# Part of the attention sum moved from VectorE to accumulating DMAs in a planned one-core kernel

## The chip, the cores and the metric

The kernel runs on one core of a Trainium2 chip. The core has a matrix engine (TensorE, PE in the profile, with its weight loads as PEld), a vector engine (VectorE, DVE), an engine for element functions and copies (ScalarE, ACT), a general one (GpSimd, POOL) and one that only issues transfers (SyncE, SP). Sixteen DMA engines move data. DMAs can be issued from SP, ACT and POOL; each of these takes its instructions in order. A DMA with `accum_op=ALU.add` adds what it reads to what lies at its destination; in this kernel all of those are issued from POOL.

The metric is device time in microseconds (us), as the median of several runs. Before the change it is 262.89 (three runs, 261.79 to 262.96).

## The reference

A block of a transformer with its two halves side by side. `x` is 2048 positions of 640 values, in bfloat16.

```python
xn = layernorm(x)                            # over the 640 values
q, k, v = split(xn @ wqkv)                   # 32 heads of 20
# attention: each position sees 8 positions: itself and 2, 4, ... 14 before it
logits[s, w] = sum_d q[s, d] * k[s - 2 * w, d] * 20 ** -0.5     # -1e9 where s - 2 * w < 0
o[s, :] = sum_w softmax(logits)[s, w] * v[s - 2 * w, :]
out = x + o @ wo + ((xn @ w_gate) * (xn @ w_up)) @ w_down       # 1536 inner values
```

## The kernel before

**Tiles and chunks.** The 2048 positions are 16 tiles of 128, and 4 chunks of 4 tiles (512 positions). Per chunk the kernel does, in this order on TensorE: the q and k projections (`qk`, L419), the v projection (`vproj`, L452), the gate and up products (`glu`, L677: 12 blocks f, each with 5 matmuls for gate and 5 for up), and the down projection (`down`, L728) with the output projection of the attention added into the same bank (L731). Chunks overlap: q, k and v of chunk c+2 are made after `down` of chunk c, so the attention of a chunk has most of a stage's time on the other engines.

**Attention of a chunk c.** VectorE multiplies q with shifted k (`products`, L520): 8 products, two into each of four buffers `pw`. Each product still has 5 blocks of 128 lanes to be summed per head. `fold` (L496) sums blocks on VectorE, in steps: a first one from 5 blocks to 3 (128x2048), a second to 2 and a third to 1 (128x1024 each); `LEVELS[c]` says how many steps. What is left is summed by TensorE in `logits` (L537), with a constant matrix `Ek`: 4 matmuls per block that is left. There are two groups of logits in a chunk, g = 0 and 1, each over two of the `pw` buffers. ScalarE copies the result out of PSUM (L552), and a transposing DMA, issued from SP, turns it into `LT` with positions on the partitions. Then VectorE takes the maximum (L578 to L582), ScalarE the exponential (L587), VectorE normalises (L595 to L600), twice per chunk, for two tiles each.

**The weighted sum over the 8 offsets.** For each tile, `av(t)` loads 8 shifted copies of v into a buffer `v8` (128 x 8 x 640, from the DRAM tensor `vD`, issued from SP, 1280 KB). VectorE weights them (L635, 128x5120), adds copies 4 to 7 to 0 to 3 (`tree`, L644, 128x2560), and then 2 to 2 and 1 to 1 (`tree2`, L648, L650). The result is transposed by a DMA from SP to `oT`, which `down` needs. `pw` and `v8` share five buffers named `pv`.

**Around it.** `vproj` evicts v from PSUM on ScalarE (L458) into one of three buffers `v_t`, and POOL stores it to `vD` (L473). The layer norm has its statistics on VectorE (L251 to L259), the power and, from tile 8 on, a shift `ns` on POOL (L265, L312) and the application on VectorE or, from tile 8 on, on ScalarE (L315). VectorE makes `hT` = gate x up (L693), 12 per chunk; TensorE starts `down` of a chunk's first tile when 10 of them are there, and needs the last two some 4 us later. For tiles 0 to 13 `out` is first seeded with x, chunk by chunk (`seed`, L709, DRAM to DRAM, from POOL), and `y` is then added to it by an accumulating DMA (L772, from POOL; the buffers `y` are two). Tiles 14 and 15 take x into SBUF (`load_xr`, L703) and are added on VectorE.

**What sets the order.** The code first collects steps, each with an engine, a cost, an occupation of the engine, what it depends on and what it must come after; `Plan.order` (L48) then places them in a list, engine by engine, always the step that is ready, with the earliest due time first. A step marked `urgent` (the logits) goes before all others that are ready, and `margin` lets what follows on another engine count as ready only so much later. The order that results is what the engines get; on the chip each engine takes its instructions in that order and waits where an input is not there yet. PE's matmuls other than the logits form one chain (`pe_main`).

Of the kernel before, what the change touches and what calls it, by code (L numbers as in the profile page):

```python
# [31 lines left out]
class Plan:  # L32
# [8 lines left out]
    def add(self, eng, cost, fn, deps=(), occ=None, after=(), kb=0):  # L41
        s = Step(eng, cost, fn, deps, occ, after)
        s.kb = kb
        s.idx = len(self.steps)
        self.steps.append(s)
        return s
# [51 lines left out]
def kernel(  # L98
# [381 lines left out]
    FO = {}  # L480
    PW, LL, LE, SS, DD, AA, O16, OE, V8, DT = {}, {}, {}, {}, {}, {}, {}, {}, {}, {}

    LEVELS = (1, 2, 3, 3)
    FOLDER = ('DVE', 'DVE', 'DVE', 'DVE')
    LEFT = (tuple(range(KT)), (0, 1, KT - 1), (0, KT - 1), (0,))
    HALVES = ((0, 2, 2, 4), (0, 1, 1, 2), (0, 1, KT - 1, KT))
# [19 lines left out]
    def products(c, hf):  # L506
        for j in range(4):
            i = 4 * hf + j
            u = i // 2

            def mul(u=u, j=j):
                if j % 2 == 0:
                    new(("pw", c, u), [P, 4, KT, HS], BF, "pv", 5)
                o = T["pw", c, u][:, 2 * (j % 2) : 2 * (j % 2) + 2, :, :]
                lo = hf * HS
                qh = T["q", c][:, :, lo : lo + HS]
                kh = T["k", c][:, :, lo + DIL * j : lo + DIL * j + HS]
                qh = bass.AP(tensor=qh.tensor, offset=qh.offset, ap=[list(qh.ap[0]), [0, 2], *[list(x) for x in qh.ap[1:]]])
                kh = bass.AP(tensor=kh.tensor, offset=kh.offset, ap=[list(kh.ap[0]), [4 * DIL, 2], *[list(x) for x in kh.ap[1:]]])
                nc.vector.tensor_tensor(o, qh, kh, ALU.mult)  # L520

            m = 8 * c + i
            w = [LL.get(2 * c - 1), O16.get(4 * c - 4), O16.get(4 * c - 3), O16.get(4 * c - 2)][u]
            PW[m] = add("DVE", 1.48, mul, [*Q[c], *Kk[c], w], occ=1.395, after=[PW.get(m - 1) if i else V8.get(4 * c - 1)])
            if j % 2:
                FO[4 * c + u] = fold(c, u)
        LASTPW[c] = PW[m]

    def logits(c, g):
        n = 2 * c + g  # L530

        def lg():
            l = new(("lps", c, g), [P, 512], F32, "pl", 2, psum)
            left = LEFT[LEVELS[c]]
            for i in left:
                for j in range(4):
                    nc.tensor.matmul(l[H * j : H * (j + 1), :], lhsT=Ek[:], rhs=T["pw", c, 2 * g + j // 2][:, 2 * (j % 2) : 2 * (j % 2) + 2, i, :],  # L537
                                     start=(i == left[0]), stop=(i == left[-1]), tile_position=(0, H * j),
                                     skip_group_check=True)

        took = 0.022 + 0.2195 * len(LEFT[LEVELS[c]])
        LL[n] = add("PE", took + 0.13, lg, [FO[2 * n], FO[2 * n + 1], LL.get(n - 1), LE.get(n - 2), CE], occ=took)
        LL[n].urgent = True
        LL[n].margin = 0.9

        def ev():
            L = new(("L", c, g), [P, 2, 2, P], BF, "L", 2)
            ps = T["lps", c, g]
            if n == 0:
                head = ps[:].rearrange("p (o s) -> p o s", o=2)[:, :, 0:HALO]  # L550
                nc.vector.tensor_tensor(head, head, negm[:], ALU.add)
            nc.scalar.copy(L[:].rearrange("p t o s -> p o t s"), ps[:].rearrange("p (o t s) -> p o t s", o=2, t=2))  # L552

        LE[n] = add("ACT", 0.585, ev, [LL[n], SS.get(n - 2), CM], occ=0.5)

        def tr():
            lt = new(("LT", n), [P, 2, W, H], BF, "LT", 2)
            out = lt[:].rearrange("p t (o w) h -> p (t o) (w h)", o=2)
            nc.sync.dma_start_transpose(out=out, in_=T["L", c, g][:].rearrange("p t o s -> p (t o s)"))

        early = [SPLAST[0]] if c == 0 else []
        SS[n] = SPLAST[0] = add("SP", 3.5, tr, [LE[n], DD.get(n - 2)], occ=1.25, after=early, kb=160)
# [62 lines left out]
    def load_out():  # L625
        WL["o"] = SPLAST[0] = add("SP", 8, wo_load, after=[SPLAST[0]], occ=2.7, kb=1100)

    def av(t):
        n, u = divmod(t, 2)
        if t > 2:  # L630
            load_v8(t)

        def mul():
            v = T["v8", t]
            nc.vector.tensor_tensor(  # L635
                v[:].rearrange("p w (j h) -> p w j h", j=Dh, h=H),
                v[:].rearrange("p w (j h) -> p w j h", j=Dh, h=H),
                T["a", n][:, u, :, None, :].to_broadcast([P, W, Dh, H]),
                ALU.mult,
            )  # L640

        def tree():
            v = T["v8", t]
            nc.vector.tensor_tensor(v[:, 0:4, :], v[:, 0:4, :], v[:, 4:8, :], ALU.add)  # L644

        def tree2():
            v = T["v8", t]
            nc.vector.tensor_tensor(v[:, 0:2, :], v[:, 0:2, :], v[:, 2:4, :], ALU.add)  # L648
            o = new(("o", t), [P, D], BF, "o", 2)
            nc.vector.tensor_tensor(o[:], v[:, 0, :], v[:, 1, :], ALU.add)  # L650

        a = add("DVE", 2.82, mul, [AA[n], V8[t]], occ=2.735)
        b = add("DVE", 1.485, tree, [a], occ=1.4)

        def tr():
            o = new(("oT", t), [P, KT, P], BF, "oT", 4)
            nc.sync.dma_start_transpose(out=o[:], in_=T["o", t][:])

        O16[t] = add("DVE", 1.35, tree2, [b, OE.get(t - 2)], occ=1.26)
        OE[t] = add("SP", 2.8, tr, [O16[t], DT.get(t - 4)], occ=1.3, kb=200, after=[V8[2]])  # L660
        if t == 0:
            SPLAST[0] = OE[0]
            load_out()
# [32 lines left out]

    XR, OB, CP = {}, {}, {}
    DIRECT = NT - 2

    def load_xr(t):  # L700
        def fn():
            x = new(("xr", t), [P, D], BF, "x", 5)
            nc.gpsimd.dma_start(out=x[:], in_=x_flat[t * P : (t + 1) * P, :])  # L703
        XR[t] = add("POOL", 2.6, fn, [VS[6]], occ=0.5, after=[HT[t // CH, 3 + t % CH]])

    def seed(c):
        def fn():
            rows = slice(c * CS, min((c + 1) * CS, DIRECT * P))
            nc.gpsimd.dma_start(out=out_flat[rows, :], in_=x_flat[rows, :])  # L709
        CP[c] = add("POOL", 6.0, fn, [VS[6]], occ=0.6, after=[HT[c, 3]])  # L710

    def down(t):
        c, q = divmod(t, CH)
        if t >= DIRECT:
            load_xr(t)
        if q == 0:
            seed(c)
        evs = []
        last = t == NT - 1
        at = [0, 512, D] if last else [0, NS, D]  # L720
# [107 lines left out]
    def between(c, work):  # L828
        for q in range(CH):
            work(q)  # L830
            if c < NCH:
                ln(c * CH + q)
                transposes(c * CH + q)
# [18 lines left out]
    for c in range(NCH):  # L852
        attention(c)
        glu(c)
        between(c + 2, lambda q: down(c * CH + q))
        if c + 2 < NCH:
            halo(c + 2)
            qk(c + 2, 0, CS)
            for q in range(CH):
                vproj((c + 2) * CH + q)  # L860
# [33 lines left out]
```

## Time and profile before

One execution was profiled. Its time was 263.27 us, of which the span from the first to the last instruction is 261.6; the granted TensorE clock was 1.000 throughout.

| what | value |
|---|---|
| median of the runs | 262.89 us |
| profiled execution, and its span | 263.27 us, 261.6 us |
| DVE: product L520 (32 times) | 1485 ns each |
| DVE: weighting L635 (16) | 2820 ns |
| DVE: first sum over offsets L644 (16) | 1486 ns |
| DVE: later sums L648, L650 (16 each) | 822, 492 ns |
| DVE: fold of 128x2048 and of 128x1024 (16, 20) | 1218, 683 ns |
| POOL: store of y, issue, and to landing (14) | 879 ns, 3.6 to 7.3 us |
| SP: load of v8, to landing (16) | 10.1 us, median |
| POOL: seed of `out`, to landing (4) | 5.1 to 12.5 us |
| DMA queues' share of the 16 engines, SP and POOL | 50.6%, 16.5% |

How to read it: the page gives each engine's busy time, then the chain of work that ended last, then groups of instructions by line. A duration on VectorE includes some 0.08 us in which the next instruction, if it does not need the result, has already begun. A bracket such as [0.77 <-ACT v_t L458] is idle time of the engine before that instruction, with what ended it. A busy TensorE has matmuls that overlap, so the distance from one start to the next is used for sums: 0.216 us for 512 columns, 0.136 for 320.

### The profile page before, as it was taken

Reading aid. Unit: us, or ns where it says so; the run is one execution under the profiler, and the core shown is the slowest. Engines: PE = TensorE matmul, PEld = TensorE weight load, DVE = VectorE, ACT = ScalarE, POOL = GpSimd, SP = SyncE. Lnnn points to the kernel's source line nnn. Section 1 sums busy time; section 2 is a strip of 40 time slices with the busy share of each in tenths; the row PEclk is TensorE's granted clock in tenths of the full one; section 3 lists DMA queues with packets and bytes.
Section 4 is the critical chain, followed back from the end, with each engine's and each line's share of the span. In section 5 each row is a group of like instructions: output and inputs, shape, how many; then the busy total and the mean of one; then the engine's idle time right before and its main releaser. Section 6 shows DMA issues by size and latency. Waiting matters only on the chain.

```text
span 261.6 us, 3920 instructions
## 1 busy us (share of the span) xinstructions
PE 252.9 (97%) x1451; PEld 141.3 (54%) x1470; DVE 229.9 (88%) x336; ACT 121.7 (47%) x233; POOL 44.8 (17%) x82
## 2 busy tenths in 40 slices
PE   6999999999999999899999999999999999999795
PEld 2655555444677546344477745544457744445563
DVE  5883998999999999799999987999999953999971
ACT  2657566856221468675521167275532144752100
POOL 4541004200042116700011110210001230000110
DMA  7998994999998505997149536971154369940361
GB/s 210 343 200 262 397 325 121 393 351 255 227 179 208 93 20 160 379 257 81 28 84 224 97 45 212 379 259 25 25 143 110 29 93 221 363 141 3 44 82 50
DMA packets 51507, 46.54 MB, mean 178 GB/s; under 512 B 24626, under 2 KB 49472, under 8 KB 51424
## 3 DMA queue, kind: packets, MB, share of 16 engines
q1 hardware_dynamic: 46704, 37.10, 50.6%
q0 software_dynamic: 3184, 8.05, 16.5%
q10 hardware_dynamic: 1600, 1.15, 1.4%
q8 instruction: 11, 0.18, 0.3%
q14 instruction: 8, 0.07, 0.1%
HBM read 35.39 MB, written 7.55 MB: 164 GB/s over the span
## 4 chain that ended last, share of the span: by engine, by line
PE 57%; DVE 30%; DMA 9%; issue 2%; ACT 1%; POOL 0%; SPq 0%; ACTq 0%
PE ps L677 18%; PE ps L728 14%; PE ps L419 12%; DVE pv L635 7%; PE ps L731 6%; PE ps L452 5%; DVE pv L520 4%; DMA LT<-L 4%; DVE pv L644 3%; DMA vD<-v_t 3%; DVE pv L496 3%; DVE hT L693 3%; DVE pv L648 2%; DMA x<-in_A_x_dram 2%; DVE st L251 2%
## 5 line engine op out<-in xcount | busy, mean ns | idle before, releaser
L677 PE MATMUL ps<-xnT,wg 128*128 128x512 bf16 x230 | 59.1, 379 | 1.3 <-ACT v_t L458 0.8
L677 PE MATMUL ps<-xnT,wu 128*128 128x512 bf16 x238 | 59.5, 379 | 0.1
L728 PE MATMUL ps<-wd,hT 128*128 128x320 bf16 (+2 forms) x383 | 57.7, 299 | 1.7 <-DVE hT L693 1.6
L520 DVE TENSOR_TENSOR pv<-q,k 128x2560 bf16<-128x2560 bf16 x32 | 45.7, 1485 | 4.4 <-ACT k L426 4.4
L728 PEld LDWEIGHTS <-hT 128*128 128x128 bf16 x384 | 37.1, 98 | 18.1 <-DVE hT L693 2.5
L635 DVE TENSOR_TENSOR pv<-pv,a 128x5120 bf16<-128x5120 bf16 x16 | 45.1, 2820 | 0.1
L677 PEld LDWEIGHTS <-wg 128*128 128x128 bf16 x240 | 23.2, 98 | 29.1 <-issue 1.9
L677 PEld LDWEIGHTS <-wu 128*128 128x128 bf16 x240 | 23.5, 98 | 28.3
L743 ACT COPY y<-ps 128x320 f32<-128x320 f32 x28 | 11.5, 427 | 54.6 <-PE ps L731 32.2
L682 ACT CAST us<-ps 128x512 bf16<-128x512 f32 x48 | 28.3, 590 | 17.1 <-PE ps L677 17.0
L682 ACT CAST gs<-ps 128x512 bf16<-128x512 f32 x48 | 28.3, 591 | 16.8 <-PE ps L677 16.7
L772 POOL DMA_DIRECT2D out_dram<-y x14 | 12.3, 879 | 120.0 <-ACT y L743 119.6
L496 DVE TENSOR_TENSOR pv<-pv 128x1024 bf16<-128x1024 bf16 (+1 forms) x36 | 30.9, 921 | 0.0
L731 PE MATMUL ps<-wo,oT 128*128 128x320 bf16 (+2 forms) x160 | 27.0, 299 | 0.0
L644 DVE TENSOR_TENSOR pv<-pv 128x2560 bf16<-128x2560 bf16 x16 | 23.8, 1486 | 0.1
L452 PE MATMUL ps<-wv,xnT 128*128 128x320 bf16 x160 | 23.2, 299 | 0.4 <-ACT xnT L365 0.4
L693 DVE TENSOR_TENSOR hT<-gs,us 128x512 bf16<-128x512 bf16 x48 | 19.3, 419 | 4.1 <-ACT us L682 4.1
L419 PE MATMUL ps<-xnT,wk 128*128 128x512 bf16 x98 | 22.6, 380 | 0.1
L419 PE MATMUL ps<-xnT,wq 128*128 128x512 bf16 x96 | 22.2, 379 | 0.2
L452 PEld LDWEIGHTS <-xnT 128*128 128x128 bf16 x160 | 15.3, 98 | 7.3 <-ACT xnT L365 0.5
L731 PEld LDWEIGHTS <-oT 128*128 128x128 bf16 x160 | 15.5, 98 | 6.2
L419 PEld LDWEIGHTS <-wk 128*128 128x128 bf16 x100 | 11.5, 118 | 10.3 <-issue 1.1
(59 smaller groups left out, 194.8 us busy)
## 6 DMA issues: line engine op xcount, KB each, us to landing
pv<-vD SPq DMA_DIRECT2D x16, 1280.0 KB, 10.1
vD<-v_t POOLq DMA_DIRECT2D x16, 160.0 KB, 5.2
out_dram<-y POOLq DMA_DIRECT2D x14, 160.0 KB, 3.9
wg<-in_B_w_gate_dram SPq DMA_DIRECT2D x1, 1920.0 KB, 8.0
wu<-in_B_w_up_dram SPq DMA_DIRECT2D x1, 1920.0 KB, 12.3
wd<-in_B_w_down_dram SPq DMA_DIRECT2D x1, 1920.0 KB, 12.3
out_dram<-in_A_x_dram POOLq DMA_DIRECT2D x3, 640.0 KB, 6.7
x<-in_A_x_dram SPq DMA_DIRECT2D x11, 160.0 KB, 4.8
```

The costliest lines, as they stand in the source:

```text
L419: nc.tensor.matmul(T[key][:, 0:n], lhsT=(wk if r else wq)[:, i, :].rearrange("p (c b) -> p c b", b=KT)[:, :, j], rhs=T["xnT", c][:, i, lo ...
L452: nc.tensor.matmul(T["psv", t, n][:, 0:NS], lhsT=T["xnT", c][:, i, q * P : (q + 1) * P], rhs=wv[:, i, n * NS : (n + 1) * NS], start=(i == ...
L496: nc.vector.tensor_tensor(w[:, :, lo:hi, :], w[:, :, lo:hi, :], w[:, :, a:b, :], ALU.add)
L520: nc.vector.tensor_tensor(o, qh, kh, ALU.mult)
L635: nc.vector.tensor_tensor(v[:].rearrange("p w (j h) -> p w j h", j=Dh, h=H), v[:].rearrange("p w (j h) -> p w j h", j=Dh, h=H), T["a", n][ ...
L644: nc.vector.tensor_tensor(v[:, 0:4, :], v[:, 0:4, :], v[:, 4:8, :], ALU.add)
L677: nc.tensor.matmul(ps[:], lhsT=(wu if r else wg)[:, i, f * P : (f + 1) * P], rhs=T["xnT", c][:, i, :], start=(i == 0), stop=(i == KT - 1))
L682: nc.scalar.copy(s[:], T[key][:])
L693: nc.vector.tensor_tensor(h[:], T["gs", c, f][:], T["us", c, f][:], ALU.mult)
L728: nc.tensor.matmul(ps, lhsT=T["hT", c, f][:, q * P : (q + 1) * P], rhs=wd[:, f, sl], start=(f == 0), stop=(f == FT - 1 and not wo_part))
L731: nc.tensor.matmul(ps, lhsT=T["oT", t][:, g, :], rhs=wo[:, g, sl], start=False, stop=(g == KT - 1 and f1 == FT))
L772: nc.gpsimd.dma_start(out=out_flat[t * P : (t + 1) * P, :], in_=T["y", t][:], accum_op=ALU.add)
```

## The change

Five edits:

1. The first sum over the offsets (`tree`) of tiles 4 to 14 is no longer made by VectorE but by two accumulating DMAs from POOL, each adding 128 x 2 x 640 values inside the buffer `v8`. Tiles 0 to 3 and 15 stay as they are.
2. The products of chunk 1 are folded to one block, as those of chunks 2 and 3 are (`LEVELS`).
3. In chunks 1 to 3 the first group of logits also waits for the folds of the second, so the two follow each other on TensorE; the planner's costs and margins for them change. In every chunk the fifth product comes after the folds of the second buffer.
4. Seeds of chunks 1 to 3 are issued a stage earlier: a one-element copy on POOL (`gate`) waits for the ninth `hT` of the chunk before.
5. The loads of x for tiles 14 and 15 come after the last seed.

```diff
-    LEVELS = (1, 2, 3, 3)
+    LEVELS = (1, 3, 3, 3)
...
-            PW[m] = add("DVE", 1.48, mul, [*Q[c], *Kk[c], w], occ=1.395, after=[PW.get(m - 1) if i else V8.get(4 * c - 1)])
+            PW[m] = add("DVE", 1.48, mul, [*Q[c], *Kk[c], w], occ=1.395, after=[(FO[4 * c + 1] if i == 4 else PW.get(m - 1)) if i else V8.get(4 * c - 1)])
...
+    PAIRED = (1, 2, 3)
...
-        took = 0.022 + 0.2195 * len(LEFT[LEVELS[c]])
-        LL[n] = add("PE", took + 0.13, lg, [FO[2 * n], FO[2 * n + 1], LL.get(n - 1), LE.get(n - 2), CE], occ=took)
+        alone = not (g and c in PAIRED)
+        took = 0.022 + 0.2195 * len(LEFT[LEVELS[c]]) + (0.19 if alone else 0.0)
+        LL[n] = add("PE", took + 0.13, lg, [FO[2 * n], FO[2 * n + 1], FO[4 * c + 3] if c in PAIRED else None, LL.get(n - 1), LE.get(n - 2), CE], occ=took)
         LL[n].urgent = True
-        LL[n].margin = 0.9
+        LL[n].margin = 0.9 if alone else 0.0
...
+    BY_DMA = (4, 5, 6, 7, 8, 9, 10, 11, 12, 13, 14)
...
-        b = add("DVE", 1.485, tree, [a], occ=1.4)
+        def tree_dma():
+            v = T["v8", t]
+            for n in range(2):
+                nc.gpsimd.dma_start(out=v[:, 2 * n : 2 * n + 2, :], in_=v[:, 4 + 2 * n : 6 + 2 * n, :], accum_op=ALU.add)
+
+        if t in BY_DMA:
+            b = add("POOL", 6.5, tree_dma, [a], occ=1.6)
+        else:
+            b = add("DVE", 1.485, tree, [a], occ=1.4)
...
+    SEED_AT = 8
+    SEED = {}
...
-        XR[t] = add("POOL", 2.6, fn, [VS[6]], occ=0.5, after=[HT[t // CH, 3 + t % CH]])
+        XR[t] = add("POOL", 2.6, fn, [CP[NCH - 1]], occ=0.5)
...
-        CP[c] = add("POOL", 6.0, fn, [VS[6]], occ=0.6, after=[HT[c, 3]])
+        if c == 0:
+            CP[c] = add("POOL", 6.0, fn, [VS[6]], occ=0.6, after=[HT[c, 3]])
+            return
+
+        def gate():
+            g = new(("gate", c), [P, 1], BF, "gate", 1)
+            nc.gpsimd.tensor_copy(g[0:1, 0:1], T["hT", c - 1, SEED_AT][0:1, 0:1])
+
+        SEED[c] = add("POOL", 0.2, gate, [HT[c - 1, SEED_AT]])
+        CP[c] = add("POOL", 6.0, fn, [SEED[c]], occ=0.85)
...
-        if q == 0:
-            seed(c)
...
+        if c == 0:
+            seed(0)
+        if c + 1 < NCH:
+            seed(c + 1)
```

In the changed kernel's order of instructions, VectorE has the same first 112 steps but for one statistics step that comes earlier; TensorE has the logits of chunk 1 after all 50 matmuls of `qk(2)` (before: after 30 and after 45), those of chunk 2 after 10 matmuls of `qk(3)` (before: 15 and 25), and those of chunk 3 in the middle of `down` of chunk 2, with three tile halves still to go (before: one just after that `down` and one 10 matmuls into the gate and up products). On VectorE products of the next chunk are drawn forward between the weightings and the later sums. Several other steps (hT, another weighting, a normalising) stand between a tile's weighting and its later sums.

## The prediction

> **What bounds the kernel now.** I read the page first (busy shares, chain, groups), then the waits of TensorE, then the timelines of TensorE (PE), VectorE (DVE), GpSimd (POOL) and SyncE (SP), then DMA landings. First the page's busy time of each engine, then two waits (us in total, times, longest):
>
> ```profile
> PE 252.9 (97%) x1451; PEld 141.3 (54%) x1470; DVE 229.9 (88%) x336; ACT 121.7 (47%) x233; POOL 44.8 (17%) x82
> PE ps L728 <- DVE hT L693: 1.6, 2, 1.3
> PE ps L677 <- ACT v_t L458: 0.8, 1, 0.8
> ```
>
> PE hardly idles: from 12 us to its last matmul at 258.8 only 2.3 us of waits. In its order of time (start, us, what, and in brackets the idle time before it with what ended it):
>
> ```profile
> 93.08 0.62 PE L537 MATMUL pl<-pv,Ek 128*32 128x512 bf16 x8
> 93.63 3.44 PE L419 MATMUL ps<-xnT,wk 128*128 128x512 bf16 x14
> 109.35 1.24 PE L677 MATMUL ps<-xnT,wg 128*128 128x512 bf16 x5 [0.77 <-ACT v_t L458]
> ...
> 211.34 0.40 PE L537 MATMUL pl<-pv,Ek 128*32 128x512 bf16 x4
> 211.67 1.25 PE L677 MATMUL ps<-xnT,wg 128*128 128x512 bf16 x4
> 239.67 0.31 PE L728 MATMUL ps<-wd,hT 128*128 128x320 bf16 x1 [0.27 <-DVE hT L693]
> 244.00 2.55 PE L728 MATMUL ps<-wd,hT 128*128 128x320 bf16 x16 [1.30 <-DVE hT L693]
> ```
>
> A logits group (L537) opens a small hole: in chunk 1 the group of 8 starts 0.09 us after the matmul before it should be through (0.216 us a piece) and holds PE 0.55, so 0.64. The two stalls at the end are DVE running late in chunk 3, and the chain tells why: a transposing DMA of the logits that took 7.22 us where its like take 2.4 (a line of the chain; that tile's landings; DVE in time).
>
> ```profile
> 212.43 7.22 DMA LT<-L
> DMA to landing us min/median/max: 2.4/2.5/7.2
> 219.67 0.29 DVE L578 TENSOR_TENSOR m<-LT 128x256 bf16<-128x256 bf16 x1 [4.59 <-DMA LT<-L]
> ```
>
> Beside it ran a seed of `out` (issued 212.70, 6.72 us), two loads of x and a store. So time is to be won in: logits holes, the 0.77, and 1.57 at the end. DVE is the other long queue, and whatever makes it late at a logits group stops PE.
>
> **The change part by part.** PE first, without new waits. Logits of chunk 1 cost 0.64 and 0.68, of chunk 2 together 1.22 (wq starts 149.40, wk 156.01, less 25 x 0.216), of chunk 3 0.43 twice: 3.40. Each pair is now 8 matmuls in a row, like one of chunk 1's groups: 3 x 0.66 = 1.98. That saves 1.42.
>
> DVE's work. Rows (start to start): product L520 1.40, fold L496 of 2048 1.135, of 1024 0.60, weighting L635 2.73, first sum L644 1.40, the two later sums 1.27, hT 0.335, max group 1.41, normalising 2.3, and 0.115 more where an instruction reads what the one before wrote. Eleven first sums go (15.4), four folds of 1024 come (2.4). But DVE is not the end by its sum; it counts where PE meets it. I lay DVE's new order out from 76.98, where chunk 1's products began. One bn_stats (0.40) has moved ahead of that: 77.4.
>
> Chunk 1: 8 x 1.40 + 4 x 1.135 + 8 x 0.60 + 0.45 for dependence = 21.0, so folds end at 98.4. PE is through its 50 matmuls at 86.52 + 50 x 0.216 = 97.3 and now waits for all four folds: start 98.5, a **new wait of 1.2**. Pair to 99.15, vproj 5.43, gate/up starts at 104.6 (before: 104.09).
>
> The stall at 109.35: the v_t eviction waited for a store to vD (issued 101.45, landed 108.77), and ScalarE's queue also for `ns` on POOL, which is slow under a weighting:
>
> ```profile
> L312 POOL TENSOR_SCALAR ns<-mv,rstd x8: 257/288/2891, 20.0 to 106.0; 128x1 f32<-128x1 f32 x8
> 102.67 4.89 POOL L312 TENSOR_SCALAR ns<-mv,rstd 128x1 f32<-128x1 f32 x3
> ```
>
> Now the first weighting comes only at about 109, and the store (issued about 102.0) goes ahead of the loads of v8, which wait on SP behind the later LT transposes (102.4). Bounds: 0.94 lost as before, or nothing. I take nothing: a store with no load beside it landed in 2.1 to 2.6. That keeps 0.94 (0.77 and the pipe's refill).
>
> DVE goes on: LT lands 3.75 after the logits start (the distance in chunk 2), 102.25; two max groups, a product, normalising: 108.7; hT can follow at 109.0. From there 12 hT, 4 weightings, 1 normalising, 4 later sums, 7 products, 12 folds = 41.9: folds of chunk 2 end at 150.9. PE: 104.6 + 25.9 + 18.5 + 10 x 0.216 = 151.1. **No wait.** From there to chunk 3: logits 151.1, LT 154.9, then 48.5 of DVE work: 203.4. PE: 151.75 + 8.6 + 5.4 + 25.9 + 85 x 0.136 = 203.3, wait 0.25. Then 0.66 + 51 x 0.136 + 25.9: gate/up ends 237.05, before 238.01. In chunk 3 the logits come 7 us earlier and no seed or x load beside them, so the 1.57 at the end go: DVE has some 3 us to spare there. Sum: -1.42 - 0.94 - 1.57 + 1.2 + 0.25 = **-2.5**.
>
> The accumulating DMAs. No row shows one in SBUF. Nearest is the store of y, which accumulates too, from rows of 2560 B like these:
>
> ```profile
> L772 POOL DMA_DIRECT2D out_dram<-y x14: 856/874/917, 73.6 to 250.3; - x14
> DMA to landing us min/median/max: 3.6/3.9/7.3
> ```
>
> Two in a row cost POOL 1.75. It has that time: a pair waits on POOL for its weighting, with stores of v_t behind it, but in chunk 2 pair 8 can go at 162.9 and the store behind it is ready only at 163.7, so nothing is held. Its packets take 0.168 us a row, 8 rows on each engine. Low end: 3.64 + 0.88 = 4.5 us a pair. High end: rows twice as long, as they have twice the elements: 1.47 to the first packet, 16 x 0.336, 0.35 to land = 7.2. Under a load of v8 a y store took 7.26, so 3.6 more: up to 10.8. The new order leaves from weighting to later sum, by the rows above: tile 4 9.7, 5 7.9, 6 7.0, 7 6.8, 8 8.5, 9 7.0, 10 8.4, 11 6.8, 12 to 14 8 or more. DVE is in order: a late pair holds hT, products and folds behind it, and each us reaches PE at the next logits. Loads of v8 run until about 117 in chunk 1 and 169 in chunk 2. Tiles 6, 7, 10, 11 fall after them: no wait at 4.5 to 6.8. Tile 9 is worst: POOL is busy with vD stores till 166.0, tile 8's pair is ahead in the queue, a load beside it till 169. 4.5 to 5.5 and half of 3.6 give about 7.5 against 6.6 left. I take **1.0** for all such waits (bounds 0 and 5), since most of the pairs stand in quiet stretches.
>
> The Trainium skill, "DMA: Bandwidth & Descriptors", section "Issuing engines are not separate DMA queues", says DMAs of all issuers share 16 engines and interleave. The 7.26 beside 3.64 agrees. It speaks against freeing DVE by DMA just when v8 is loaded: with no wait at tile 9 the sum would be -2.5, by this rule -1.5.
>
> Seeds. Seed 0 stays. Seed 1 leaves 110.45 (where it took 12.5 beside loads) for 65 to 68, where the DMA queues are 99% busy; one packet of 1.66 us on each engine in front of v8 of tile 3, which landed 70.19 for a weighting at 71.34: bounds 0 and 0.6, taken 0, since POOL's `gate` must read hT while a weighting runs and so comes late (2.9 in the ns row). Seeds 2 and 3 come after the pairs of tiles 7 and 11 and delay only x transposes that have 10 us. x loads of tiles 14, 15 are as early. y stores wait in POOL behind the gate: y has two buffers, over 4 us each. SP's oT transposes wait for later sums as before; v8 of tiles 8 and 12 behind them have over 10 us. On ScalarE nothing is added.
>
> **Sum.** -2.5 + 1.0 = -1.5 on the profiled 263.27 (span 261.6 and 1.7 around it): 261.8. That run lies 0.38 above the median of 262.89, so the median forecast is 261.4.
>
> **The rivals.**
> *Late accumulation (slower).* Pairs take 9 us where loads run and 8.5 elsewhere: DVE stops about 1.7 in chunk 1 and 3.5 in chunk 2. -2.5 + 5.2 = +2.7, 265.6. It decides from 2.5 us of waits in all. For it: 7.26, and vD stores of 5 to 11 us; against: the quiet rows.
> *No change.* The wait for the vD store in chunk 1 stays: hT starts at 110.9, DVE is 1.9 later, PE waits 1.5 more at chunk 2's logits and as late at chunk 3's: -1.5 + 1.75 = +0.25, 263.1. For it: that store took 7.3, and its like in chunk 2 6.0.
> *All in time.* No wait at tile 9, perhaps none at chunk 1's logits: -2.5 to -3.7, 259.2 to 260.4.
> *POOL kept from issuing.* Each issue waits for a DVE instruction, on average half of 2.8, 2.8 a pair: 1.5 in chunk 1, 3.8 in chunk 2, so -2.5 + 5.3 = +2.8, 265.7. Against it: vD issues under a running weighting (165.08) took 0.57, as all 16 (0.54 to 0.65). The Trainium skill, "SBUF — State Buffer", section "SBUF: two separate sides", says a DVE instruction in a 2-port mode keeps GpSimd from writing descriptors; the issue rows here do not show it, the ns row shows its like for reads.
>
> **How the numbers follow.** Forecast 0.34 (-0.8 to -2.2), all in time 0.14, no change 0.20, late 0.27, POOL 0.05. One per cent of spread in the runs shown lets 0.5% (1.3 us) tell from no change. Faster: four fifths of the forecast and all in time, 0.41. Same: a fifth of the forecast, no change, a fifth of late, 0.32. Slower 0.27. The range goes from the middle of all in time, 259.6, to late, 265.4; the forecast alone 260.7 to 262.1.
>
> **What would show it.** Right: three groups of 8 on L539 with no hole but about 1 us ahead of chunk 1's; LT at 2.4 us in chunk 3; no PE wait for hT in the last 25 us; DVE waiting for pv's DMA at L653 only once or twice. Wrong: DVE waits at L653 of over 2 us in chunk 2, PE waiting at L539 for DVE in chunks 2 and 3, pairs landing later than 8 us.

## Result and profile after

The changed kernel takes 266.43 us (median of four runs, 264.76 to 266.96), the kernel before 262.34 on the same chip: a ratio of 1.0144, 95% interval 1.0111 to 1.0176, slower by 1.4%. Ratios leave out executions in which the chip was in a slower state. The forecast was 261.4, with a range up to 265.4, so sign and range both failed. The profiled execution is the shortest of the four (264.76 us, span 263.0, 1.8 around it); the three others take 1.4 to 2.2 us more. Between this execution and the one profiled before (263.27) lie only 1.5 us, so the profile shows less than the whole loss.

First the page of the changed kernel: busy time of each engine, the kind of queue that GpSimd's DMAs use (packets, MB, share of 16 engines), and the shares of the chain that ended last.

```profile
PE 252.2 (96%) x1444; PEld 141.7 (54%) x1462; DVE 217.6 (83%) x329; ACT 121.9 (46%) x233; POOL 62.9 (24%) x107
...
q0 software_dynamic: 6352, 15.26, 29.6%
...
PE 39%; DVE 38%; issue 14%; DMA 4%; POOL 3%; ACT 1%; POOLq 0%; DVEq 0%
```

GpSimd's queue took 29.6% of the sixteen engines' span, and 16.5% before: by these shares (an estimate) some 35 us more of all sixteen, about 3.2 us for each tile's pair of DMAs. VectorE (DVE) has 12.3 us less work (229.9 before), and yet it is now 38% of the chain (30% before), and TensorE (PE) 39% (57%; 49% in the second profile below). An engine with less to do decides more of the time: it must be standing for something. The waits say for what (us in total, times, longest):

```profile
DVE pv L653 <- DMA pv<-pv: 6.4, 5, 2.6
...
PE pl L539 <- DVE pv L496: 4.7, 4, 1.9
...
PEld L539 <- DVE pv L496: 0.9, 1, 0.9
...
PE ps L750 <- DVE hT L706: 0.5, 1, 0.5
```

VectorE waits at the later sum (L653) for the accumulating DMAs, and TensorE waits at the logits (L539) for VectorE's folds (L496). The wait for hT, 1.6 us at the end before, is down to 0.5 and stands elsewhere (134.89). TensorE in its order of time, at the three pairs of logits groups:

```profile
97.40 0.40 PE L539 MATMUL pl<-pv,Ek 128*32 128x512 bf16 x4
98.36 0.40 PE L539 MATMUL pl<-pv,Ek 128*32 128x512 bf16 x4 [0.56 <-DVE pv L496]
98.69 5.61 PE L452 MATMUL ps<-wv,xnT 128*128 128x320 bf16 x40
...
152.26 0.40 PE L539 MATMUL pl<-pv,Ek 128*32 128x512 bf16 x4 [0.78 <-DVE pv L496]
154.19 0.40 PE L539 MATMUL pl<-pv,Ek 128*32 128x512 bf16 x4 [1.53 <-DVE pv L496]
...
206.16 0.40 PE L539 MATMUL pl<-pv,Ek 128*32 128x512 bf16 x4
208.44 0.40 PE L539 MATMUL pl<-pv,Ek 128*32 128x512 bf16 x4 [1.88 <-DVE pv L496]
```

The pairs are not eight matmuls in a row. The first group starts once TensorE reaches it and its own two folds are done (the dependence that the change adds orders the plan and holds nothing on the chip); the second waits in place for its own. From the last matmul ahead to the first behind, chunk 1 loses 1.4 us, chunk 2 3.2 (151.3 to 154.5), chunk 3 2.7 (206.1 to 208.8): 7.3 in all, against 3.4 for the six separate groups before. In chunk 3 the matmuls of `down` that follow at 208.77 need nothing of these groups, but TensorE runs its written order.

VectorE's stops ahead of that, and the pairs' landings (all 22 DMAs, from issue):

```profile
110.10 0.42 DVE L706 TENSOR_TENSOR hT<-gs,us 128x512 bf16<-128x512 bf16 x1 [1.64 <-ACT us L695]
...
129.60 0.82 DVE L653 TENSOR_TENSOR pv<-pv 128x1280 bf16<-128x1280 bf16 x1 [0.21 <-DMA pv<-pv]
...
137.45 0.82 DVE L653 TENSOR_TENSOR pv<-pv 128x1280 bf16<-128x1280 bf16 x1 [1.22 <-DMA pv<-pv]
...
177.48 0.82 DVE L653 TENSOR_TENSOR pv<-pv 128x1280 bf16<-128x1280 bf16 x1 [2.03 <-DMA pv<-pv]
...
233.79 0.83 DVE L653 TENSOR_TENSOR pv<-pv 128x1280 bf16<-128x1280 bf16 x1 [2.59 <-DMA pv<-pv]
```

```profile
DMA to landing us min/median/max: 3.6/6.2/9.7
```

The four are tiles 6, 7, 9 and 13. From the end of a tile's weighting to the landing of its second DMA, the trace has 6.2 to 7.1 us for tiles 4 to 6 and 11, 8.0 to 8.6 for 7, 8, 10 and 14, 9.2 for 9, 9.6 for 12 and 10.8 for 13. Tile 7's (landed 137.36) ran beside a seed (issued 130.47). Not all of the 6.4 us reach TensorE: 2.9 of them, at tiles 12 and 13, come after the last logits, and behind 208.44 TensorE has no stall in either profile of this kernel.

### The profile page after: what moved, and what is told of

Same layout as the page of the kernel before. It is cut to its first block, busy times and chain, and to the rows that moved or that the text cites. A ratio compares the mean times of both kernels' runs of the same rounds, so it can differ in the third digit from the quotient of the medians.

```text
span 263.0 us, 3949 instructions
## 1 busy us (share of the span) xinstructions
PE 252.2 (96%) x1444; PEld 141.7 (54%) x1462; DVE 217.6 (83%) x329; ACT 121.9 (46%) x233; POOL 62.9 (24%) x107
## 3 DMA queue, kind: packets, MB, share of 16 engines
q0 software_dynamic: 6352, 15.26, 29.6%
## 4 chain that ended last, share of the span: by engine, by line
PE 39%; DVE 38%; issue 14%; DMA 4%; POOL 3%; ACT 1%; POOLq 0%; DVEq 0%
PE ps L690 19%; DVE pv L520 12%; DVE pv L496 9%; PE ps L750 7%; DVE pv L640 5%; PE ps L419 4%; PE ps L452 4%; DMA pv<-pv 3%; DVE hT L706 3%; PE ps L753 3%; DVE pv L649 2%; DVE pv L653 2%; PE ps L242 2%; POOL out_dram L794 1%; DMA LT<-L 1%
## 5 line engine op out<-in xcount | busy, mean ns | idle before, releaser
L520 DVE TENSOR_TENSOR pv<-q,k 128x2560 bf16<-128x2560 bf16 x32 | 46.3, 1485 | 3.4 <-ACT k L426 3.4
L496 DVE TENSOR_TENSOR pv<-pv 128x1024 bf16<-128x1024 bf16 (+1 forms) x40 | 34.3, 900 | 0.4
L661 POOL DMA_DIRECT2D pv<-pv x22 | 19.2, 1033 | 31.5 <-PE ps L690 14.5
L753 PEld LDWEIGHTS <-oT 128*128 128x128 bf16 x160 | 15.4, 98 | 6.8 <-DMA oT<-o 0.5
L653 DVE TENSOR_TENSOR pv<-pv 128x1280 bf16<-128x1280 bf16 x16 | 13.1, 821 | 6.4 <-DMA pv<-pv 6.4
## 6 DMA issues: line engine op xcount, KB each, us to landing
wd<-in_B_w_down_dram SPq DMA_DIRECT2D x1, 1920.0 KB, 12.3
```

The costliest lines, as they stand in the source:

```text
L496: nc.vector.tensor_tensor(w[:, :, lo:hi, :], w[:, :, lo:hi, :], w[:, :, a:b, :], ALU.add)
L661: nc.gpsimd.dma_start(out=v[:, 2 * n : 2 * n + 2, :], in_=v[:, 4 + 2 * n : 6 + 2 * n, :], accum_op=ALU.add)
L753: nc.tensor.matmul(ps, lhsT=T["oT", t][:, g, :], rhs=wo[:, g, sl], start=False, stop=(g == KT - 1 and f1 == FT))
```

## Experiments

Two theories stood at first. **A**: the accumulating DMAs land late, VectorE, which works in order, stands for them, and its late folds stop TensorE. **B**: the pairing itself loses, since two groups now stand where TensorE must wait for four folds. A third, **C**: the DMAs' traffic slows other transfers. Times are medians in us; a ratio is to the kernel before on the same chip, with its 95% interval. Kernels sent together were compared on one chip; between groups the ratio is the number to compare, and 1% of it is 2.6 us.

**The changed kernel again**, no edit.

> The changed kernel once more, with a second profile. Expected: 266.4 us (265 to 267), and in the profile the same three marks as in the first: 5 to 8 us of VectorE waits at L653 for the accumulating DMAs, 4 to 7 us of TensorE waits at L539 for the folds, pairs that land 6 to 11 us after the weighting. If the waits are much smaller in a profile of about 266.4 us, the loss has another place.

266.37 us, ratio 1.0151 (1.0108 to 1.0193). The marks are there: 5.9 us at L653, 5.5 at L539, pairs with a median of 6.5 us from issue. One thing is new. Stretches of 1 us in chunk 1 of this second profile; columns: stretch, its length, PE busy (instructions), then the same for PEld, DVE, ACT and POOL, then the granted TensorE clock, DMA share, GB/s:

```profile
97.00:98.00 1.00, 0.57 (x6) 0.19 (x4) 1.00 (x3) 0.57 (x1) 0.00 (x0) 1.00 0.00 0
98.00:99.00 1.00, 0.23 (x4) 0.00 (x0) 0.98 (x2) 0.60 (x2) 0.00 (x0) 1.00 0.00 0
99.00:100.00 1.00, 0.24 (x4) 0.10 (x4) 0.96 (x4) 0.00 (x0) 0.00 (x0) 1.00 0.00 0
100.00:101.00 1.00, 1.00 (x11) 0.61 (x8) 1.00 (x4) 0.61 (x2) 0.80 (x2) 0.91 0.65 131
101.00:102.00 1.00, 1.00 (x5) 0.60 (x4) 1.00 (x4) 1.00 (x2) 0.02 (x1) 0.50 0.00 0
102.00:103.00 1.00, 1.00 (x6) 0.59 (x4) 0.93 (x6) 0.65 (x2) 0.25 (x1) 0.50 0.65 131
103.00:104.00 1.00, 1.00 (x6) 0.54 (x5) 0.86 (x6) 0.36 (x2) 0.98 (x3) 0.50 0.50 110
104.00:105.00 1.00, 1.00 (x8) 0.69 (x7) 0.97 (x2) 0.52 (x3) 1.00 (x2) 0.88 1.06 390
```

TensorE stood twice at the logits (0.43 and 1.53 us), and behind that its clock was halved for some 3.4 us. The 40 matmuls of the v projection took 7.28 us here and 5.61 in the first profile: 1.67 us that no wait names. So a stall can be paid a second time. It explains neither the loss nor the spread, though: of this kernel's ten executions in both groups of runs, seven have a mean clock of 0.994 or less, and the three at 0.999 or 1.000 took 264.76, 266.21 and 266.96 us.

**The first sum on VectorE again**, the rest as changed.

```diff
-    BY_DMA = (4, 5, 6, 7, 8, 9, 10, 11, 12, 13, 14)
+    BY_DMA = ()
```

> BY_DMA is empty: VectorE makes the first sum of every tile again, the levels, the pairing and the seeds stay as changed. The planner then puts chunk 2's logits at another place (15 matmuls earlier or later in the q/k stage). Theory A (late accumulating DMAs hold VectorE in its order, and VectorE's late folds hold TensorE): 6.4 us of waits at L653 leave and 11 x 1.4 = 15.4 us of work come; before carried that work with no such stalls, so 261 to 264 us, no more than 1 us of TensorE waits at L539. Theory B (the pairing itself: the logits now wait for four folds): 265.5 to 267, waits at L539 stay at 4 us or more. Theory C (traffic and issues of the accumulating DMAs slow the other transfers): 261 to 264 too.

266.25 us, 1.0122 (1.0084 to 1.0161). All the accumulating DMAs are gone, and the time stays. A and C as I had put them (261 to 264) are misses. B expected the time but not the place: TensorE's waits at L539 are only 1.8 us, and larger ones stand at other places (all with idle time in the brackets from 96 us on, but the 0.1 at chunk 2's logits):

```profile
98.33 0.40 PE L539 MATMUL pl<-pv,Ek 128*32 128x512 bf16 x4 [0.98 <-DVE pv L496]
...
110.47 1.24 PE L690 MATMUL ps<-xnT,wg 128*128 128x512 bf16 x5 [1.88 <-ACT v_t L458]
...
137.89 2.21 PE L750 MATMUL ps<-wd,hT 128*128 128x320 bf16 x15 [1.46 <-DVE hT L706]
...
219.40 0.40 PE L539 MATMUL pl<-pv,Ek 128*32 128x512 bf16 x4 [0.84 <-DVE pv L496]
...
247.11 2.55 PE L750 MATMUL ps<-wd,hT 128*128 128x320 bf16 x16 [1.55 <-DVE hT L706]
```

**No first sum at all** for tiles 4 to 14: copies 4 to 7 are left out of their sums.

```diff
         def tree_dma():
             v = T["v8", t]
-            for n in range(2):
-                nc.gpsimd.dma_start(out=v[:, 2 * n : 2 * n + 2, :], in_=v[:, 4 + 2 * n : 6 + 2 * n, :], accum_op=ALU.add)
+            return
```

> The two accumulating DMAs of each of tiles 4 to 14 are not issued and nothing takes their place: copies 4 to 7 are left out of the sums of these tiles. The order on the engines stays. Theory A: the 6.4 us of waits at L653 are gone, VectorE ends chunk 2's and chunk 3's folds some 2 us earlier, the waits at L539 fall from 4.7 to about 1, the time by 3 to 5 us, to 261.5 to 263.5. Theory B: 265.5 to 267, the waits at L539 stay over 3.5. Theory C: a gain as by A.

262.06 us, 0.9960 (0.9928 to 0.9991): 1.9% under the changed kernel. TensorE's waits at L539 fell to 0.6 us. With no sum to make, chunk 3's pair runs as forecast, eight in a row:

```profile
152.11 0.40 PE L539 MATMUL pl<-pv,Ek 128*32 128x512 bf16 x4 [0.39 <-DVE pv L496]
...
204.08 0.62 PE L539 MATMUL pl<-pv,Ek 128*32 128x512 bf16 x8
```

**The same traffic, nobody waits for it.**

```diff
-                nc.gpsimd.dma_start(out=v[:, 2 * n : 2 * n + 2, :], in_=v[:, 4 + 2 * n : 6 + 2 * n, :], accum_op=ALU.add)
+                nc.gpsimd.dma_start(out=v[:, 4 + 2 * n : 6 + 2 * n, :], in_=wo[:, 2 * n : 2 * n + 2, :], accum_op=ALU.add)
```

> The same two DMAs of 320 KB per tile from the same queue at the same place, but they add two slices of wo into copies 4 to 7, which nobody reads, instead of copies 4 to 7 into 0 to 3: the later sum (L653) waits for no DMA, only the next user of the buffer does. Copies 4 to 7 are left out of the sums of tiles 4 to 14. Theory A: within 1 us of the kernel without the first sum, 261.5 to 264. Theory C (traffic and issues): within 1 us of the changed kernel, 265.5 to 267, with no waits at L653. Theory B: 265.5 to 267 in both.

263.86 us, 1.0046 (1.0017 to 1.0075): between the two. Of the 5.0 us from no sum (0.9960) to the sum by DMA (1.0151, all three on one chip), the DMAs as traffic make 0.86%, 2.3 us, and the waiting for them, with all that follows a wait, 1.05%, 2.7 us; by the intervals each part is known to some 1.1 and 1.3 us. A and C share the loss. One place of the traffic is plain in the profile: the load of v8 for tile 15 took 24.9 us (15.3 without any first sum), VectorE stood for it, and hT came late:

```profile
236.28 2.82 DVE L640 TENSOR_TENSOR pv<-pv,a 128x5120 bf16<-128x5120 bf16 x1 [5.32 <-DMA pv<-vD]
...
242.84 0.31 PE L750 MATMUL ps<-wd,hT 128*128 128x320 bf16 x1 [1.26 <-DVE hT L706]
```

At the logits of chunks 2 and 3, 1.4 us of stalls are left (0.4 without any first sum). Two more stalls of this profile, 0.97 at chunk 1's logits and 1.10 for v_t at 109.85, are not the traffic's: the first of these DMAs is issued at 115.36.

**Each part of the change alone**, on the kernel before. The edits are the parts of the diff above: the tuple BY_DMA with its branch; LEVELS; PAIRED with the logits' dependence on the fourth fold, their cost and margin; and the seeds with their gate and the later loads of x. The order of the products was not run alone.

> The kernel before with one part of the change: the first sum of tiles 4 to 14 by accumulating DMAs. So far: the changed kernel at 266.4 us loses 2.5 us by the waits for the pairs and 1.8 us by their traffic (the runs traffic_aside and no_first_sum), but gives nothing back when VectorE sums again (sum_on_dve). Theory A1 (the DMA sum and the VectorE sum cost about the same here, another part of the change lost the time): 261 to 263.5, within 1 us of before. Theory A2 (the DMA sum by itself loses, 4 us as in the changed kernel, and VectorE's sum loses in the changed kernel only because of the rest): 265 to 267.

271.52 us, 1.0334 (1.0298 to 1.0370): a loss of 9 us, far over the upper end of both expectations (263.5 and 267). VectorE's waits at its later sum, and TensorE's for hT behind it, in this kernel (its lines stand three lower):

```profile
DVE pv L650 <- DMA pv<-pv: 12.2, 5, 4.1
...
PEld L738 <- DVE hT L703: 6.7, 4, 2.1
...
PE ps L738 <- DVE hT L703: 5.5, 4, 1.8
```

TensorE also stood 2.38 us for v_t at 177.25. On GpSimd, in order, the stores to vD of that chunk stood behind the pairs of tiles 8 and 9: issued from 168.74 (163.72 before), they landed from 176.70 (169.68 before), and an eviction to v_t waited 5.60 us for a buffer.

> The kernel before with one part of the change: chunk 1's product blocks are folded to one (three levels). That adds 4 folds on VectorE (0.63 us each by their elements) ahead of chunk 1's logits and takes 8 matmuls from TensorE. Theory E (the added fold is the loss: VectorE is late in chunk 1 and stays late): 264.5 to 266.5. Otherwise 262 to 263.5.

262.98 us, 1.0010 (0.9979 to 1.0041): no difference.

> The kernel before with one part of the change: in chunks 1 to 3 the two groups of logits stand together, after all four folds. Theory B (the pairing is the loss: TensorE waits for the later folds): 264.5 to 266.5, with TensorE waits at L539 of over 3 us. Otherwise 261 to 263.

265.78 us, 1.0119 (1.0076 to 1.0161): the time that B expected, but with waits at the logits of some 1 us, not over 3; the largest stall is 2.08 at 244.30, for hT. The profiled execution is the fastest of the six (263.57), so its waits stand for less than the median's loss.

> The kernel before with one part of the change: seeds 1 to 3 are issued in the gate/up stage of the chunk ahead, behind a small copy on GpSimd. Theory D (the seeds, 2.5 MB to 3 MB of traffic for chunk, now collide with loads of the gate/up stage): 264 to 266. Otherwise 261.5 to 263.

261.33 us, 0.9952 (0.9931 to 0.9973): a gain of 1.2 us, a little below what was expected. In chunk 3 no seed runs beside the transposing DMA of the logits any more, and the two stalls for hT at the end are gone; what is left is 1.53 us at 109.53 for v_t.

**The changed kernel without the pairing.**

```diff
-    PAIRED = (1, 2, 3)
+    PAIRED = ()
```

> The changed kernel without the pairing: each group of logits comes when its own two folds are done. Sums by DMA, levels and seeds as changed. So far pairing alone cost 3.3 us (only_pairing), the DMA sum alone 9.0 (only_dma_sum), the seeds alone gained 1.2, the levels alone nothing. Theory B (what the changed kernel loses is the pairing): 262.5 to 264. Theory A (the late pairs, which hold VectorE whatever the logits' place): 265.5 to 268, with VectorE waits at L653 of 5 us or more.

267.73 us, 1.0173 (1.0130 to 1.0216). A's expectation of the time holds (4.9 us of waits at L653, a little under the 5 named), B's is a miss: with the sums by DMA, taking the pairing away gains nothing.

**DMA sum and moved seeds**, on the kernel before.

> The kernel before with two parts of the change: the first sums by DMA and the moved seeds. With the old seeds, seeds 1 and 2 were issued right behind the pairs of tiles 7 and 11, which then took 9 to 12 us. Theory F (the 9 us of the DMA sum alone were mostly this collision with the seeds): 263 to 266. Theory A2 (the pairs are late by themselves): 268 to 271.

270.03 us, 1.0291 (1.0241 to 1.0340). F is a miss. In the kernel with the DMA sum alone the second DMAs of two pairs did land 10.7 and 10.8 us after issue, with a seed issued half a us behind each (tiles 5 and 11; the expectation names 7 in place of 5), but tile 13's took 11.1 with no seed beside it, and moving the seeds gives back 0.4%, no more than the seeds gain alone.

**Moved seeds and levels**, without the two parts that lose.

> The two parts of the change that did not lose: the moved seeds (1.2 us faster alone) and the levels (0.5 us slower alone, less than its uncertainty). If they add up: 261 to 262, faster than both kernels. If the levels bring chunk 1's fold late beside the seeds: 262.5 to 264.

261.31 us, 0.9939 (0.9910 to 0.9968): faster than both kernels, by 0.6% than before, not to be told from the seeds alone. Its page and chain, and the one stall of TensorE that is left behind 96 us:

```profile
PE 253.3 (98%) x1462; PEld 141.4 (55%) x1462; DVE 231.6 (89%) x340; ACT 121.5 (47%) x233; POOL 45.6 (18%) x85
...
PE 89%; DVE 8%; issue 1%; DMA 1%; ACT 0%; DVEq 0%
```

```profile
241.48 2.55 PE L750 MATMUL ps<-wd,hT 128*128 128x320 bf16 x16 [1.27 <-DVE hT L706]
```

VectorE is busier than before by 1.7 us, and decides 8% of the time.

**Planned for later landings.** The planner's cost of a tile's DMA sum decides how far behind the weighting it writes the later sum.

```diff
-            b = add("POOL", 6.5, tree_dma, [a], occ=1.6)
+            b = add("POOL", 9.5, tree_dma, [a], occ=1.6)
```

> The changed kernel, planned with a cost of 9.5 us for a tile's DMA sum instead of 6.5: the later sums (L653) come later in VectorE's order, TensorE's order stays. Theory A (VectorE stands at L653 for pairs that are later than planned): waits at L653 fall from 6 us to under 2, TensorE's at L539 from 5 to 2 to 3, 263.5 to 265. Theory B (pairing): waits at L539 stay over 4, 265.5 to 267.

266.08 us, 1.0120 (1.0074 to 1.0166). The waits at L653 fall to 0.4 us as A expected, and the time does not follow; B's time and its 4 us at L539 hold. TensorE still stands 0.35 and 1.53 us at chunk 1's logits and 2.22 at chunk 3's, and 0.99 at 140.04 for a transposed o, which comes later now; its clock was halved behind two of the stalls (from 100 and from 209 us), which only two of the six executions show in their mean clock. So planning for the wait at L653 did not win its price back; that the later sum and what hangs on it are then late by plan is my reading, which no run isolates.

**TensorE kept at work in the pair's stall.** Twelve matmuls between the two groups, overwritten by the second.

```diff
             left = LEFT[LEVELS[c]]
+            for j in list(range(4)) * (3 if g and c in PAIRED else 0):
+                nc.tensor.matmul(l[H * j : H * (j + 1), :], lhsT=Ek[:], rhs=T["pw", c, j // 2][:, 2 * (j % 2) : 2 * (j % 2) + 2, 0, :],
+                                 start=True, stop=True, tile_position=(0, H * j), skip_group_check=True)
             for i in left:
```

> The changed kernel, with 12 matmuls of 128 x 512 (1.2 us) between the two logits groups of chunks 1 to 3, whose results are overwritten by the second group. They need only the first group's blocks and so run in the 1.5 to 1.9 us in which TensorE stands for the second group's folds. Theory G (a stall of some 2 us halves TensorE's clock for 3.5 us in most executions, 1.7 us a time): no window below 0.9 of the clock behind the logits, the median falls from 266.4 to 264.5 to 265.5, near the undisturbed profile. If the clock plays no part: 266.2 to 267.

266.38 us, 1.0108 (1.0052 to 1.0164), beside 1.0151 (1.0108 to 1.0193) without. The mean clock is 0.999 or 1.000 in all six executions, where it was 0.994 or less in five of six without, but the median is not lower and the intervals overlap: G's time is a miss, and the other expectation holds. So the halved clock is not where the changed kernel loses; how much it adds is hidden by the time of the twelve matmuls themselves. Stalls of 0.88 and 1.58 us stayed in front of groups.

**Neither pairing nor first sum**: copies 4 to 7 left out for tiles 4 to 14.

> The changed kernel without the pairing and without the first sum of tiles 4 to 14 (copies 4 to 7 are left out of these tiles' sums). Beside it the paired kernel without that sum took 262.1 us. Theory B1 (pairing costs by itself): 259 to 260.5, some 2 us less than paired. Theory B2 (pairing costs only where VectorE is late, since it leaves TensorE no slack at the logits): within 1 us of the paired one, 261.3 to 262.8.

262.30 us, 0.9982 (0.9941 to 1.0022). B2 holds: without the sum, pairing costs nothing that can be measured (0.9960 paired).

**Three tiles back on VectorE**, those with the longest waits.

```diff
-    BY_DMA = (4, 5, 6, 7, 8, 9, 10, 11, 12, 13, 14)
+    BY_DMA = (4, 5, 6, 8, 10, 11, 12, 14)
```

> The changed kernel with the first sum of tiles 7, 9 and 13 on VectorE again, the three tiles for whose pairs VectorE stood 1.2, 2.0 and 2.6 us in the profile; each costs VectorE 1.4 us of work instead. Theory A (these waits are the loss): waits at L653 under 1.5 us in all, 264 to 265.5. If only the sum of VectorE's time counts (5.8 us of waits against 4.2 of work): 265.5 to 266.5. If the other pairs turn late instead: 266 to 267.

264.80 us, 1.0054 (1.0019 to 1.0090): nearly 1% under the changed kernel, as A expected. The list of the longest waits has none at L653 any more. Tile 13's wait had held up no matmul in the first profile, so it is more likely tiles 7 and 9 that gained; the run does not part them. What remains in the profile is 1.00 us at chunk 1's logits and 2.60 us in gate/up for v_t, with the clock halved behind it.

**One tile by DMA in the fastest version** (moved seeds and levels).

```diff
-    BY_DMA = ()
+    BY_DMA = (14,)
```

> The fastest version so far (moved seeds and levels, 261.3 us) with the DMA sum for tile 14 alone. In its profile one TensorE stall of 1.27 us is left, for chunk 3's last gate/up product; 1.4 us less on VectorE ahead of it could end it: 260 to 261. If the pair is late (8.5 us in the changed kernel) and VectorE stands for it: 261.5 to 263.

264.14 us, 1.0029 (1.0000 to 1.0058), against 0.9939 without: even one tile loses. VectorE does not stand for the DMA here. The planner, with the first sum gone from VectorE, wrote two weightings in a row (5.55 us from 233.56) ahead of three products hT, so ScalarE stood 3.01 us for a buffer and TensorE here, and its clock was halved behind it:

```profile
239.51 0.98 PE L750 MATMUL ps<-wd,hT 128*128 128x320 bf16 x3 [1.57 <-DVE hT L706]
240.32 0.97 PE L753 MATMUL ps<-wo,oT 128*128 128x320 bf16 x5
241.08 2.87 PE L750 MATMUL ps<-wd,hT 128*128 128x320 bf16 x10
```

Ten matmuls of 128x320 in 2.87 us; in the changed kernel ten take 1.52 (243.65). But eight of the twelve executions have full clock, and their median is still 264.0, so the clock is not the loss. The stall is only 0.3 us longer than the fastest version's 1.27, and the two kernels ran on different chips: what costs the 2.4 us (0.90% by the ratios) is not shown.

**The pairing where VectorE sums.** The fastest version differs from the changed kernel with sums on VectorE not only by the pairing, but by two small edits that came with it: the products of the second half wait for the second fold, and the planner's cost of a logits group is 0.19 us more. So the changed kernel without pairing and without DMA sums, both edits in, beside the paired one:

```diff
-    PAIRED = (1, 2, 3)
+    PAIRED = ()
-    BY_DMA = (4, 5, 6, 7, 8, 9, 10, 11, 12, 13, 14)
+    BY_DMA = ()
```

> The changed kernel without pairing and with all first sums on VectorE; the order of the products and the planner's cost of a logits group stay as changed. If the pairing is the loss: 261 to 262.5, ratio 0.993 to 1.000. If the order of the products or the planner's cost is: 265 to 267, as the paired kernel.

263.53 us, 1.0025 (0.9999 to 1.0050).

> The changed kernel with all first sums on VectorE, once more, on the same chip as unpaired_on_dve: 265.5 to 267, ratio 1.008 to 1.016.

266.22 us, 1.0148 (1.0118 to 1.0177). Neither expectation for the unpaired one holds: it lies between. The pairing costs 1.2%, 3.2 us, the same as alone on the kernel before (3.1). In the profiles the paired one has 1.3 us of stalls at the logits where the unpaired one has none, and 1.46 and 1.54 us for hT at 137 and 246 us against 0.91 and 0.55: 2.8 us, the difference of the spans (263.9 and 261.1). But the paired one also has 1.22 us for a transposed o at 80.26, ahead of the first pair, and the unpaired one 1.42 for v_t at 109.20. So folds that TensorE waits for and products of VectorE that come later are the likely places; one execution of each does not show it. The two small edits together cost 0.9%, 2.3 us, by the fastest version's 0.9939 (which was measured on another chip).

**Together.** Ratio to before, with moved seeds, three levels and the two small edits in all:

| first sum of tiles 4 to 14 | none | on VectorE | by DMA |
|---|---|---|---|
| logits unpaired | 0.9982 | 1.0025 | 1.0173 |
| logits paired | 0.9960 | 1.0122, 1.0148 | 1.0144, 1.0151 |

Unpaired, VectorE's 15.4 us of first sums cost 0.4%, 1.1 us, with intervals that overlap and on two chips; paired they cost 1.6 to 1.9%, 4.3 to 4.9 us. So much could be won by taking them off. By DMA they cost 5 us, paired or not. Pairing costs 2.5 to 3.2 us when VectorE makes the sums, and nothing that can be measured, or less, in the other columns. The change joined two parts that each lose by themselves and whose losses do not add: the DMA sum alone loses 9 us, but 4.5 with the seeds, the levels and the two small edits (1.0173; 1.0291 with the seeds only). What in the levels or the small edits takes 3 us back there is not shown.

## Why the prediction was wrong

**The accumulating DMAs (1.0 us) is the step that failed.** The price of a pair was well bounded, 4.5 to 7.2 and 10.8 contended: measured 6.2 to 10.8. The choice inside it was wrong: "most of the pairs stand in quiet stretches" holds for four of eleven, if quiet means up to 7.2. Tile 9 was the worst case in my reckoning, 7.5 of 6.6 us left; it took 9.2. Tiles 7 and 13 were taken as free, with 6.8 and 8 us of room. Tile 7's took 8.6, beside the seed that the change itself had put behind it (7.1 with the DMA sum alone, where no seed ran beside it). Tile 13's took 10.8, with tile 12's pair (landed 229.42) and a load of v8 (landed 233.87) still under way. I had asked whom the seeds delay only on the other side ("only x transposes"), not the pair in front of them. VectorE's waits were 6.4 and 5.9 us in the two profiles, and 2.9 and 3.0 of these held up no matmul. What the waiting costs the program, from the traffic experiment, is 2.7 us, within the bounds of 0 and 5, not 1.0.

**A term was missing: the traffic itself, 2.3 us.** The sum charged the pairs only for who waits for them. That they make other transfers land later had no term: the load of v8 for tile 15 took 21.7 us, 14.8 before. In the changed kernel's profile VectorE stood for tile 13's pair until 233.79, when that load landed (233.87), so the two prices lie one over the other. How the whole 2.3 us reach TensorE is not shown.

**The store of chunk 1** failed as well, but not by the pairs. It was taken to land in 2.1 to 2.6 us, with no load beside it, since the loads of v8 were to wait until 102.4. They were issued at 101.28 and 101.84, the store at 101.86, and it landed at 107.72; the first pair was issued only at 113.81. hT of chunk 1 then started at 110.10 (forecast 109.0), and at 112.31 in the second profile, which runs 1.4 us later from chunk 1's first product on. This is the rival "no change", in part.

**"No wait" in chunk 2 and 0.25 in chunk 3** followed from the first and the third: the folds were forecast for 150.9 and 203.4 and ended at 154.1 and 208.4. Of chunk 2's 3.2 us, 1.1 are the late hT, 1.4 the waits at L653 and 0.4 a wait for a transposed o (130.87); for chunk 3 tile 9's 2.0 come on top. And the pairing makes such lateness dear, which I counted only in chunk 1: the first group goes in order, and then TensorE stands for the second with nothing else written in between.

**The gains.** The late transposing DMA of chunk 3 (7.22 before) takes 2.4, and the two stalls at the end are gone: right, -1.57, and the seeds alone give 1.2 us. In front of gate/up in chunk 1, the profiled run no longer shows the stall of 0.77: right in that profile, but VectorE waits 1.64 there instead. The logits' -1.42 came only where nothing is late: 0.62 for chunk 3's eight without the sum. The kernel without the first sum has all the gains and none of the prices: 1.0 us (0.2 to 1.9) below before, where these gains came to 2.5 with the waits of 1.2 and 0.25. Between the two profiled executions alone it is 2.6 (263.27 to 260.63), but 260.63 is the third fastest of twelve, so part of that agreement is luck. In ratios the account closes by its making: -1.0 for all but the sum, +2.3 for the traffic, +2.7 for the waiting give +4.0, where the forecast had -2.5, nothing and +1.0.

**The relief of VectorE.** The prediction said that VectorE "is not the end by its sum" and counted its time only where TensorE meets it. Unpaired the table bears that out, with 1.1 us for 15.4 us less of work. With the pairing, which the change brings, the relief is worth 4.3 to 4.9, and the DMAs cost all of it.

**The rivals.** "Late accumulation" gave +2.7 and 265.6 (the range ended a little below it, at 265.4), from pairs of 8.5 to 9 us. From tile 7 on they took 8.0 to 10.8 but for tile 11's; VectorE stopped 1.4 us in chunk 1 and 2.0 in chunk 2, where the rival had 1.7 and 3.5. The measured +4.1 is this rival and the traffic; all three signs of being wrong that the prediction names were seen. "GpSimd kept from issuing" was not: the issues follow 0.3 to 0.7 us after the weighting.

Two rules of the Trainium skill bear on this. "DMA: Bandwidth & Descriptors", section "Issuing engines are not separate DMA queues", says that the DMAs of all issuers share the 16 engines. The traffic experiment agrees, with 2.3 us where I had given it one tile. "TensorE: Matmul & The Clock Gate", section "Part 1: The HAM clock gate", which the prediction did not use, says that the clock falls to half after at least one idle window of about 3.4 us, that the window runs freely, and that full rate comes back after about one busy window. The 0.50 over 3.4 us agrees. But stalls that come to 1.6 to 3.0 us sufficed here, and whether one is followed by it differs: the 0.78 and 1.53 of chunk 2 in the first profile were not.

What stays open: which of the two small edits costs the 2.3 us where VectorE sums, by which waits the traffic costs its 2.3, and how much the clock adds to an execution that pays for it.

## What to carry to other kernels

Before moving work off a busy engine, ask whether that engine decides the time where the work stands: here 15.4 us of work on an 88% busy engine cost the program 1.1 us, or over 4 with the logits paired, and the DMAs that took it over cost 5, about half as waits of an engine that works in order and half as traffic that delays other transfers. A queue's price must be read with everything that the change itself puts beside it. Two consumers written back to back need both producers on time, so pair them only where the producer has slack.

## What the runs showed of the hardware

A pair of accumulating DMAs within SBUF, 320 KB each, landed 6.2 to 7.1 us after the end of the weighting for four tiles and 8.0 to 10.8 for seven; a single one 3.6 to 9.7 from issue, median 6.2. The seven had a seed, stores, a load of v8 or the pair ahead still under way, but so had tile 4, which took 6.6 with a load of v8 beside it (landed 116.80): what makes the difference is not isolated.

Stalls of TensorE had a second price that no list of waits shows. In the profiles of seven kernels the granted clock fell to 0.50 while TensorE still had work, nine times in all. It followed one or two stalls that come to 1.6 to 3.0 us, lasted 3.4 us and so cost about 1.7 (an estimate: half of it). Stalls of 2.08 us (244.30, pairing alone) and 2.38 (177.25, DMA sum alone) passed without it. So the same stall costs once or almost twice over.
